# Squares to ScalarE, subtractions and wide sums to VectorE, and an order planned with a shared port, in a retention and MLP kernel

## The chip, the cores and the metric

The kernel runs on one core of one Trainium2 chip. The metric is the device time of one execution in microseconds; the median of three runs is given. The engines are TensorE (PE), VectorE (DVE), ScalarE (ACT), GpSimd (POOL) and SyncE (SP), which issues the transfers.

## The reference

Attention with decay in place of softmax, then an MLP with a squared ReLU, then a gated MLP with SiLU, all in float32. The 4 x 576 rows of the attention are the 2304 rows of the MLPs.

```
q, k, v: (4, 8, 576, 64);  x: (2304, 512)
scores = q @ k.T / 8;  Dmat[i, j] = gamma_h ** (i - j) for i >= j, else 0
x = ((scores * Dmat) @ v), heads side by side
h = relu(x @ w_in);  x = (h * h) @ w_out              # d_ff 2048
g = x @ w_gate;  x = (g * sigmoid(g) * (x @ w_val)) @ w_out2   # d_ff 1536
```

## The kernel before

Every float32 operand of a product is split into a high and a low part of a form that TensorE multiplies fast, and a product is three matmuls (`three`, lines 200 to 202: high by high, high by low, low by high). A split is a rounding copy on ScalarE (`hi`, line 279) and a subtraction on VectorE (`lo`, line 283); the helper `split` makes both for weights, x parts and activations.

The weights arrive as 64-bit patterns. `round32` turns them into float32 (ScalarE lines 241 and 246, VectorE lines 249 to 261), in `convert1` for the first MLP and `convert2_pair` for the second.

The stages are: attention for the first cells; the first MLP's blocks 0 and 1 (`mlp1_h`, `mlp1_act`, `mlp1_y`) with the rest of the attention between their products; its blocks 2 to 4 (`mlp1_s`); the second MLP in three passes of six tiles of 128 rows. Blocks 2 to 4 and the second MLP use Strassen's scheme, in Winograd's form: seven products instead of eight (`PRODUCTS`), with sums of weights (GpSimd, lines 326 and 405), sums of x (`sub` in `fetch_x1`, line 733, and in `fetch_x`, line 967; T1 to T4) and sums of results.

In `mlp1_s` one turn p makes two hidden blocks of 128 for 512 rows. Products go into two banks; `copy` (line 835: m1, u2, m5) and `add` (line 842) take them out, `relu` (line 848) follows on ScalarE, `square` (line 852) on GpSimd, then `hi` (ScalarE, line 860) and `lo` (VectorE, line 864). Pieces of the output product of the turn before are laid between the products. There are 96 halves of 128x256 to be squared. In blocks 0 and 1 the squares run on ScalarE already (line 669).

In the second MLP, `mlp2_gv` makes one hidden block of a pass in seven products: `copy` (ScalarE, line 1069), sums on VectorE (line 1078 c11; line 1081 c22, which product 6 waits for; line 1084 c12; lines 1094 to 1100 the gate). `act_sum` (GpSimd, line 1156) makes sums of activations; `operand` splits activations into `at` tiles; `o_piece` (lines 1217 to 1219) makes the output products, three tiles at a time, laid between the products of later blocks and, at the end of a pass, in one run. `fetch_x` loads the next pass's x and splits it into `xc` tiles; these are the same buffers that the old pass uses, so that the splitting begins with the last block of a pass. `sums_out` takes the output banks out: P1, P7, P5 and C11 copied by ScalarE (line 1258), U2, C21 and C12 added on VectorE (line 1265), and two wide sums, U3 and C22, over 128x768 in `both` (GpSimd, line 1271); then the stores (line 1278).

The order of each engine's queue is made by a planner before the program is written (`Plan`). Each operation is given with its engine, a cost in us, its dependencies and a rank; `emit` steps through time, takes for each engine the ready operation of the least rank, and writes it. TensorE's own order is a chain that follows the program text (`pe`). The costs set the order, and nothing else: the engines wait on semaphores. Sums that TensorE waits for have rank -3, activations -2, the next pass's x 4, weight conversions over 100.

Of the kernel before, what the change touches and what calls it, by code (L numbers as in the profile page):

```python
# [15 lines left out]
ALU = mybir.AluOpType  # L16
# [27 lines left out]
NA = 10  # L44
LOOK = 0.25
Y_FIRST = (0, 0, 3, 3)
TINY, HUGE = (float(np.uint32(b).view(np.float32)) for b in (0x40000000, 0x4FEFFFFF))
# [17 lines left out]
class Op:  # L65


    __slots__ = ("eng", "us", "fn", "deps", "after", "rank", "kb", "n", "out", "left", "ready", "end", "fill")

    def __init__(self, eng, us, fn, deps, after, rank, kb):  # L70
        self.eng, self.us, self.fn, self.rank, self.kb = eng, us, fn, rank, kb
        self.deps, self.after = list(deps), list(after)
        self.out, self.left, self.ready, self.end, self.fill = [], 0, 0.0, None, None


class Plan:
# [9 lines left out]

    def __call__(self, eng, us, fn, deps=(), rank=0.0, kb=0, key=None, after=()):


        o = Op(eng, us, fn, deps, after, rank, kb)  # L90
        o.n = len(self.ops)
        self.ops.append(o)
        if key is not None:
            self.named[key] = o
        return o

    def emit(self):
        waiting = {}
        for o in self.ops:
            for whole, of in ((True, o.deps), (False, o.after)):  # L100
                for d in of:
                    d = d if isinstance(d, Op) else self.named.get(d)
                    if d is not None and d is not o:
                        o.left += 1
                        d.out.append((o, whole))
            if not o.left:
                waiting.setdefault(o.eng, []).append(o)
        free, lanes, left = {}, 0.0, len(self.ops)
        while left:
            best = None  # L110
            for eng, todo in waiting.items():
                if not todo:
                    continue
                t = free.get(eng, 0.0)
# [12 lines left out]
            left -= 1  # L127
            free[o.eng] = t + o.us
            if o.kb:
                lanes = max(lanes, t + o.us + 1.3) + o.kb / 400.0  # L130
                o.end = lanes + 3.0
            else:
                o.end = t + o.us
            for x, whole in o.out:
                lag = 0.0 if x.eng == o.eng else self.LAG.get(o.eng, 0.08)
                x.ready = max(x.ready, o.end + lag if whole else t + 0.01)
                x.left -= 1
                if not x.left:
                    waiting.setdefault(x.eng, []).append(x)
# [18 lines left out]
def kernel(ctx: ExitStack, tc: tile.TileContext, units, qtab, tab, w1, w2, out):  # L158
# [75 lines left out]
    def round32(box, rank, apart=False):  # L234
# [29 lines left out]
        o2 = do("ACT", 1.16, a2, [box["load"] if apart else o1, *r_users[-1:]], rank)  # L264
        p1 = do("DVE", 1.0 if apart else 0.8, d1, [o1], rank)
        p2 = do("DVE", 1.0 if apart else 0.8, d2, [p1], rank)
        p3 = do("DVE", 0.87, d3, [o2] if apart else [p2, o2], rank)
        raw_free = do("NONE", 0.0, lambda: None, [o1, o2, p3])
        do.named["raw", box["n"]] = raw_free
        converts.append(o1)  # L270
        p4 = do("DVE", 1.34, d4, [p2, p3, o2], rank)
        r_users.append(p4)
        return st, p4

    def split(get, n, out, place, rank, deps, cols=None):
# [9 lines left out]
        h = do("ACT", 0.17 + 0.43 * n / 512, hi, deps, rank)  # L285
        return do("DVE", 0.16 + 0.53 * n / 512, lo, [h], rank)

# [25 lines left out]
    def convert_s(p, rank):  # L313
# [15 lines left out]
        ld = do("SP", 0.4, load, [wf_saved[p], f_users[-2]], rank - 20, kb=512, after=raw_loads[-1:])  # L329
        x = do("POOL", 0.87, add(2, 3, 2, ALU.add), [ld], rank)  # L330
        x = do("POOL", 0.87, add(3, 0, 3, ALU.subtract), [x], rank)
        x = do("POOL", 0.87, add(0, 2, 0, ALU.subtract), [x], rank)
        x = do("POOL", 0.87, add(1, 1, 0, ALU.subtract), [x], rank)

# [13 lines left out]
    def convert2_pair(box, f, rank, plain, summed, steps):  # L348
# [31 lines left out]
        def lo2():  # L380
# [5 lines left out]
                    [("xbdone", NB - 1), ("ysv", NB - 2)] if home == "xs" else [("ysv", NB - 1)])  # L386
        front = lambda: do("DVE", 0.69, lo(low, 0, n), [h, *low_free], rank)
        back = lambda: do("DVE", 0.43, lo(rest, n, 768), [h], rank)
        if steps is GV_SUMS:
# [12 lines left out]
        for o, x, y, op in steps:  # L402
            def add(o=o, x=x, y=y, op=op):
                w = st["fm"].rearrange("p (s n) -> p s n", s=4)
                nc.gpsimd.tensor_tensor(out=w[:, o], in0=w[:, x], in1=w[:, y], op=op)  # L405
            l = do("POOL", 0.87, add, [l if o != steps[0][0] else need[o], need[o]], rank)
        h = do("ACT", 1.03, hi2, [l], rank)
        l = do("DVE", 1.22, lo2, [h], rank)
        e = w_dram[summed, f]
# [97 lines left out]
    def att_prep(c, rank):  # L507
# [10 lines left out]
        if c not in FIRST:  # L518
            qs_op[c] = do("POOL", 1.45, qs, [A_op[c], Q_op[c]], rank, after=[ks_op[c - 1]])
        if c not in LAST:  # L520
            ks_op[c] = do("POOL", 1.25, ks, [V_op[c], tab_op], rank, after=[qs_op[c]])

# [133 lines left out]
    def mlp1_act(j, f):  # L656
# [30 lines left out]
        c = do("ACT", 0.19 + 0.43 * k, hi, [b, y_op.get(order1[i - 2]) if i > 1 else None], -2)  # L687
        hlo_op[j, f] = do("DVE", 0.16 + 0.53 * k, lo, [c], -2)

# [29 lines left out]
    def fetch_x1(j, rank):  # L719
# [10 lines left out]
        def sub(o, a, c, deps):  # L730
            eng, us = ("DVE", 0.69) if o in ("T1", "T2") else ("POOL", 1.5)
            e = nc.vector if eng == "DVE" else nc.gpsimd
            return do(eng, us, lambda: e.tensor_tensor(out=at(o), in0=at(a), in1=at(c), op=ALU.subtract), deps, rank)

# [60 lines left out]
    def mlp1_s(j, p, pieces):  # L795
# [55 lines left out]
        def square(key, half):  # L851
            return lambda: nc.gpsimd.tensor_tensor(out=st[key][:, half], in0=st[key][:, half], in1=st[key][:, half], op=ALU.mult)  # L852

        def finish(key, f, half, deps):
# [10 lines left out]

            r = do("POOL", 0.87, square(key, half), deps, -2)
            h = do("ACT", act, hi, [r, y_op.get(order1[i - 2])], -2)
            return do("DVE", 0.58, lo, [h], -2)

# [3 lines left out]
        c11 = name("s11", do("DVE", dve, add("g0", lo_half, "MB", "m1", True), [N_op[j, p, 1], m1, hlo_op.get((j, 2 * p - 3))], -3))  # L873
        r0 = do("ACT", act, relu("g0", lo_half), [c11], -2)
        e0 = finish("g0", f0, lo_half, [r0])
# [8 lines left out]
        c22 = name("s22", do("DVE", dve, add("g1", hi_half, "MA", "m5", True), [N_op[j, p, 4], m5, hlo_op.get((j, 2 * p - 2))], -3))  # L884
        r1 = do("ACT", act, relu("g1", hi_half), [c22], -2)
        e1 = finish("g1", f1, hi_half, [r1])
        product(5, "MB", [m5])
        c12 = name("s12", do("DVE", dve, add("g0", hi_half, "MB", "u2", False), [N_op[j, p, 5], u2], -3))
        r0 = do("ACT", act, relu("g0", hi_half), [c12], -2)
        e0 = finish("g0", f0, hi_half, [r0, e0])  # L890
        hlo_op[j, f0] = e0
        y(take_y[2])
        product(6, "MA", [c22])
        c21 = name("s21", do("ACT", act, relu("g1", lo_half, "MA"), [N_op[j, p, 6]], -3))
        hlo_op[j, f1] = finish("g1", f1, lo_half, [c21, e1])
        y(take_y[3])
# [53 lines left out]
    def fetch_x(b, rank):  # L950
# [14 lines left out]

        def sub(o, a, c):
            return lambda: nc.gpsimd.tensor_tensor(out=at(o), in0=at(a), in1=at(c), op=ALU.subtract)

# [16 lines left out]

        parts_in_order(part, lambda *a, deps: do("POOL", 2.4, sub(*a), deps, min(rank, 4) if b else rank), ld)
        do.named["ysdone", b] = x_chain[-1]
# [59 lines left out]
    def mlp2_gv(s, pieces):  # L1047
# [76 lines left out]
        sg = do("ACT", act, sig(0, lo_half), [c11_, ("si2", s - 1)], -2)  # L1124
        si1 = name("si1", do("DVE", dve, silu(0, lo_half), [sg], -2))
        other(0)
# [11 lines left out]
        sg = do("ACT", act, sig(1, hi_half), [c12_, sg], -2)  # L1138
        si2 = name("si2", do("DVE", dve, silu(1, hi_half), [sg], -2))
        t2_ = name("t2", do("DVE", dve, t2, [si2, c22_], -2))  # L1140
        other(2)
# [9 lines left out]
    def act_sum(b, q, out, x, y, op, deps, rank=-2):  # L1151
# [5 lines left out]

        s_op[b, q, out] = do("POOL", 1.18, go, deps, rank)

# [81 lines left out]
    def sums_out(b):  # L1241
# [27 lines left out]
        def both(name, dst, src, deps):  # L1269
            def go():  # L1270
                nc.gpsimd.tensor_tensor(out=box(dst), in0=box(dst), in1=box(src), op=ALU.add)
            c_op[b, name] = do("POOL", 2.9, go, deps, -3)

# [294 lines left out]
```

## Time and profile before

| | us |
|---|---|
| median of 3 runs | 888.45 (888.36 to 889.59) |
| the profiled execution | 887.93 |
| its span, first to last instruction | 886.1 |
| TensorE busy in it | 865.6 |
| VectorE busy | 639.2 |
| ScalarE busy | 471.6 |
| GpSimd busy | 354.5 |

The span is what the trace shows of the profiled execution; 1.8 us of its time lie around it. TensorE's busy time is a union of overlapping matmuls, so what it lacks to the span is time in which no matmul ran; it does not show whether the clock was at its full or its half level, which is in the column of the granted clock.

### The profile page before, as it was taken

Reading aid. Unit: us, or ns where it says so; the run is one execution under the profiler, and the core shown is the slowest. Engines: PE = TensorE matmul, PEld = TensorE weight load, DVE = VectorE, ACT = ScalarE, POOL = GpSimd, SP = SyncE. Lnnn points to the kernel's source line nnn. Section 1 sums busy time; section 2 is a strip of 40 time slices with the busy share of each in tenths; the row PEclk is TensorE's granted clock in tenths of the full one; section 3 lists DMA queues with packets and bytes.
Section 4 is the critical chain, followed back from the end, with each engine's and each line's share of the span. In section 5 each row is a group of like instructions: output and inputs, shape, how many; then the busy total and the mean of one; then the engine's idle time right before and its main releaser. Section 6 shows DMA issues by size and latency. Waiting matters only on the chain.

```text
span 886.1 us, 15973 instructions
## 1 busy us (share of the span) xinstructions
PE 865.6 (98%) x5995; PEld 809.3 (91%) x5995; DVE 639.2 (72%) x938; ACT 471.6 (53%) x898; POOL 354.5 (40%) x333
## 2 busy tenths in 40 slices
PE   9799999999999999999999999989999989999998
PEld 7688878999899899989999999989999989999998
DVE  4899895637878978897887878596555587555565
ACT  2767674347667667676564544463333354333353
POOL 4131205653646566556581434252122144221231
PEclk9999999999999999999999999999999999999999
DMA  9777868998989698879889998959777767775772
GB/s 359 259 272 269 313 218 258 398 375 282 367 285 352 245 344 315 289 238 341 319 311 323 301 417 317 348 196 330 273 254 259 266 206 259 262 276 214 260 261 74
DMA packets 113085, 254.84 MB, mean 288 GB/s; under 512 B 8560, under 2 KB 67696, under 8 KB 103664
## 3 DMA queue, kind: packets, MB, share of 16 engines
q1 hardware_dynamic: 113008, 253.82, 81.2%
q8 instruction: 47, 0.77, 0.3%
q14 instruction: 30, 0.25, 0.1%
HBM read 195.59 MB, written 58.20 MB: 286 GB/s over the span
## 4 chain that ended last, share of the span: by engine, by line
PE 76%; DVE 13%; issue 3%; DMA 3%; ACT 3%; POOL 2%; SPq 0%; ACTq 0%; POOLq 0%; DVEq 0%
PE gv L200 12%; PE gv L201 12%; PE gv L202 12%; PE acc L201 6%; PE acc L202 6%; PE acc L200 6%; DVE at L283 4%; PE acc L1219 3%; PE acc L1217 3%; PE acc L1218 3%; PE hps L200 3%; PE hps L202 2%; PE hps L201 2%; PE sc L528 1%; PE xs L568 1%
## 5 line engine op out<-in xcount | busy, mean ns | idle before, releaser
L200 PE MATMUL gv<-xc,w 128*128 128x384 f32 x504 | 171.6, 340 | 6.5 <-DVE m L1081 5.7
L201 PE MATMUL gv<-xc,w 128*128 128x384 f32 x504 | 170.3, 338 | 0.0
L202 PE MATMUL gv<-xc,w 128*128 128x384 f32 x504 | 170.0, 337 | 0.0
L201 PE MATMUL acc<-h,w 128*128 128x512 f32 (+1 forms) x320 | 117.8, 368 | 1.1 <-DVE h L679 0.8
L202 PE MATMUL acc<-h,w 128*128 128x512 f32 (+1 forms) x320 | 117.6, 368 | 0.2
L852 POOL TENSOR_TENSOR g<-g 128x256 f32<-128x256 f32 x96 | 86.8, 913 | 77.2 <-ACT g L848 76.5
L200 PE MATMUL acc<-h,w 128*128 128x512 f32 (+1 forms) x320 | 117.3, 367 | 0.0
L200 PEld LDWEIGHTS gv<-xc,w 128*128 128x128 f32 x504 | 94.9, 188 | 9.2 <-DVE m L1081 7.0
L201 PEld LDWEIGHTS gv<-xc,w 128*128 128x128 f32 x504 | 95.3, 189 | 0.2
L202 PEld LDWEIGHTS gv<-xc,w 128*128 128x128 f32 x504 | 95.0, 189 | 0.0
L1219 PE MATMUL acc<-w,at 128*128 128x256 f32 x288 | 81.6, 283 | 0.0
L1218 PE MATMUL acc<-w,at 128*128 128x256 f32 x288 | 81.3, 282 | 0.0
L1217 PE MATMUL acc<-w,at 128*128 128x256 f32 x288 | 81.2, 282 | 0.0
L1069 ACT COPY m<-gv 128x384 f32<-128x384 f32 x72 | 34.6, 481 | 83.1 <-PE gv L202 81.9
L1156 POOL TENSOR_TENSOR st<-g,rs 128x384 f32<-128x384 f32 x18 | 21.7, 1204 | 141.1 <-DVE rs L1100 141.1
L405 POOL TENSOR_TENSOR f<-f 128x256 f32<-128x256 f32 x72 | 66.2, 919 | 29.2 <-DVE cw L362 18.4
L202 PEld LDWEIGHTS acc<-h,w 128*128 128x128 f32 x320 | 60.1, 188 | 10.9 <-DVE w L283 1.0
L864 DVE TENSOR_TENSOR h<-g,h 128x256 fp32r<-128x256 f32 x96 | 62.6, 652 | 7.6 <-ACT h L860 7.5
L200 PE MATMUL gv<-xb,w 128*128 128x256 f32 x238 | 67.2, 282 | 0.8 <-ACT m L835 0.4
L201 PEld LDWEIGHTS acc<-h,w 128*128 128x128 f32 x320 | 60.1, 188 | 8.6 <-DVE h L679 1.3
L201 PE MATMUL gv<-xb,w 128*128 128x256 f32 x238 | 66.9, 281 | 0.1
L202 PE MATMUL gv<-xb,w 128*128 128x256 f32 x238 | 66.8, 281 | 0.0
(175 smaller groups left out, 2246.4 us busy)
## 6 DMA issues: line engine op xcount, KB each, us to landing
w<-wdS SPq DMA_DIRECT2D x36, 1024.0 KB, 5.6
raw<-w SPq DMA_DIRECT2D x34, 1024.0 KB, 7.3
w<-wdP SPq DMA_DIRECT2D x36, 768.0 KB, 7.0
w<-ws SPq DMA_DIRECT2D x94, 256.0 KB, 4.9
w<-wdOP SPq DMA_DIRECT2D x54, 256.0 KB, 4.8
w<-wdOS SPq DMA_DIRECT2D x18, 768.0 KB, 7.4
ws<-cw SPq DMA_DIRECT2D x16, 512.0 KB, 7.2
wdS<-cw SPq DMA_DIRECT2D x12, 512.0 KB, 5.3
```

The source lines that it names most:

```text
L200: nc.tensor.matmul(ps, lhsT=wh, rhs=xh, start=first, stop=False, skip_group_check=onto)
L201: nc.tensor.matmul(ps, lhsT=wh, rhs=xl, start=False, stop=False, skip_group_check=onto)
L202: nc.tensor.matmul(ps, lhsT=wl, rhs=xh, start=False, stop=last, skip_group_check=onto)
L283: nc.vector.tensor_tensor(out=t[:, 1], in0=get(), in1=t[:, 0].bitcast(F32), op=ALU.subtract)
L405: nc.gpsimd.tensor_tensor(out=w[:, o], in0=w[:, x], in1=w[:, y], op=op)
L852: return lambda: nc.gpsimd.tensor_tensor(out=st[key][:, half], in0=st[key][:, half], in1=st[key][:, half], op=ALU.mult)
L864: nc.vector.tensor_tensor(out=t[:, 1, half], in0=st[key][:, half], in1=t[:, 0, half].bitcast(F32), op=ALU.subtract)
L1069: nc.scalar.copy(out=st[name], in_=late[bank][:, :HALF])
L1156: nc.gpsimd.tensor_tensor(out=o, in0=i, in1=k, op=op)
L1217: nc.tensor.matmul(ps, lhsT=ah, rhs=wh, start=product not in ONTO and q == 0 and off == 0, stop=False, skip_group_check=True)
L1218: nc.tensor.matmul(ps, lhsT=ah, rhs=wl, start=False, stop=False, skip_group_check=True)
L1219: nc.tensor.matmul(ps, lhsT=al, rhs=wh, start=False, stop=q == NQ - 1, skip_group_check=True)
```

## The change

The squares of the first MLP's blocks 2 to 4 move from GpSimd to ScalarE, as a second activation right behind the ReLU (`gate`). The x subtractions T3 and T4 of `fetch_x1` and all four of `fetch_x` move from GpSimd to VectorE, and so do the wide sums U3 and C22 at the end of each pass (`both`). The planner learns that GpSimd and some of VectorE's operations (`lock`: those with two inputs in SBUF and some others) slow each other: while both run, each proceeds at the fraction that `SHARE` gives, and an operation that was already placed on the other engine is put off accordingly (`grow`). With that, several costs that held a mean of the slowed times are lowered: weight sums from 0.87 to 0.75 us, activation sums from 1.18 to 1.02, the steps of `round32` and the attention's GpSimd products likewise. Besides what is shown, `lock=True` is set on the low parts of all splits, on `silu` and on `t2`. The products, their order on TensorE and the transfers are not edited.

```diff
+SHARE = {"DVE": 0.5, "POOL": 0.62}
...
-    __slots__ = ("eng", "us", "fn", "deps", "after", "rank", "kb", "n", "out", "left", "ready", "end", "fill")
-
-    def __init__(self, eng, us, fn, deps, after, rank, kb):
+    __slots__ = ("eng", "us", "fn", "deps", "after", "rank", "kb", "n", "out", "left", "ready", "end", "fill", "lock")
+
+    def __init__(self, eng, us, fn, deps, after, rank, kb, lock):
         self.eng, self.us, self.fn, self.rank, self.kb = eng, us, fn, rank, kb
         self.deps, self.after = list(deps), list(after)
-        self.out, self.left, self.ready, self.end, self.fill = [], 0, 0.0, None, None
+        self.out, self.left, self.ready, self.end, self.fill, self.lock = [], 0, 0.0, None, None, lock or eng == "POOL"
...
-        free, lanes, left = {}, 0.0, len(self.ops)
+        free, lanes, left, run = {}, 0.0, len(self.ops), {}
+
+        def grow(o, end):
+            for x, whole in o.out:
+                if whole:
+                    x.ready = max(x.ready, x.ready if x.end else end + (0.0 if x.eng == o.eng else 0.08))
+            o.end = free[o.eng] = end
+
...
+            if o.lock:
+                other = run.get("POOL" if o.eng == "DVE" else "DVE")
+                us = o.us
+                if other and other[0].end > t + 1e-9:
+                    x, since, both, left_x = other
+                    left_x -= max(0.0, min(t, both) - since) * SHARE[x.eng] + max(0.0, t - max(both, since))
+                    first = min(us / SHARE[o.eng], left_x / SHARE[x.eng])
+                    ends = [t + first + max(0.0, w - first * SHARE[e]) for w, e in ((us, o.eng), (left_x, x.eng))]
+                    grow(x, ends[1])
+                    run[x.eng] = x, t, t + first, left_x
+                    run[o.eng] = o, t, t + first, us
+                    free[o.eng] = ends[0]
+                else:
+                    run[o.eng] = o, t, t, us
             if o.kb:
                 lanes = max(lanes, t + o.us + 1.3) + o.kb / 400.0
                 o.end = lanes + 3.0
             else:
-                o.end = t + o.us
+                o.end = free[o.eng]
...
-        p1 = do("DVE", 1.0 if apart else 0.8, d1, [o1], rank)
-        p2 = do("DVE", 1.0 if apart else 0.8, d2, [p1], rank)
-        p3 = do("DVE", 0.87, d3, [o2] if apart else [p2, o2], rank)
+        p1 = do("DVE", 0.69, d1, [o1], rank, lock=True)
+        p2 = do("DVE", 0.69, d2, [p1], rank, lock=True)
+        p3 = do("DVE", 0.75, d3, [o2] if apart else [p2, o2], rank, lock=True)
...
-        p4 = do("DVE", 1.34, d4, [p2, p3, o2], rank)
+        p4 = do("DVE", 1.24, d4, [p2, p3, o2], rank)
...
-        x = do("POOL", 0.87, add(2, 3, 2, ALU.add), [ld], rank)
+        x = do("POOL", 0.75, add(2, 3, 2, ALU.add), [ld], rank)
...
-            eng, us = ("DVE", 0.69) if o in ("T1", "T2") else ("POOL", 1.5)
-            e = nc.vector if eng == "DVE" else nc.gpsimd
-            return do(eng, us, lambda: e.tensor_tensor(out=at(o), in0=at(a), in1=at(c), op=ALU.subtract), deps, rank)
+            eng, us = ("DVE", 0.69)
+            return do(eng, us, lambda: nc.vector.tensor_tensor(out=at(o), in0=at(a), in1=at(c), op=ALU.subtract), deps, rank, lock=True)
...
-            return lambda: nc.gpsimd.tensor_tensor(out=st[key][:, half], in0=st[key][:, half], in1=st[key][:, half], op=ALU.mult)
+            return lambda: nc.scalar.activation(out=st[key][:, half], in_=st[key][:, half], func=ACTF.Square)
+
+        def gate(key, half, deps, bank=None):
+            r = do("ACT", act, relu(key, half, bank), deps, -3 if bank else -2)
+            return r, do("ACT", act, square(key, half), [r], -2)
...
-            r = do("POOL", 0.87, square(key, half), deps, -2)
-            h = do("ACT", act, hi, [r, y_op.get(order1[i - 2])], -2)
-            return do("DVE", 0.58, lo, [h], -2)
+            h = do("ACT", act, hi, [*deps, y_op.get(order1[i - 2])], -2)
+            return do("DVE", 0.42, lo, [h], -2, lock=True)
...
-        r0 = do("ACT", act, relu("g0", lo_half), [c11], -2)
+        _, r0 = gate("g0", lo_half, [c11])
...
-        c21 = name("s21", do("ACT", act, relu("g1", lo_half, "MA"), [N_op[j, p, 6]], -3))
-        hlo_op[j, f1] = finish("g1", f1, lo_half, [c21, e1])
+        c21, r1 = gate("g1", lo_half, [N_op[j, p, 6]], "MA")
+        name("s21", c21)
+        hlo_op[j, f1] = finish("g1", f1, lo_half, [r1, e1])
...
-        def sub(o, a, c):
-            return lambda: nc.gpsimd.tensor_tensor(out=at(o), in0=at(a), in1=at(c), op=ALU.subtract)
+        def sub(o, a, c, deps):
+            eng, us = ("DVE", 0.96)
+            return do(eng, us, lambda: nc.vector.tensor_tensor(out=at(o), in0=at(a), in1=at(c), op=ALU.subtract), deps, min(rank, 4) if b else rank, lock=True)
...
-        parts_in_order(part, lambda *a, deps: do("POOL", 2.4, sub(*a), deps, min(rank, 4) if b else rank), ld)
+        parts_in_order(part, sub, ld)
...
-                nc.gpsimd.tensor_tensor(out=box(dst), in0=box(dst), in1=box(src), op=ALU.add)
-            c_op[b, name] = do("POOL", 2.9, go, deps, -3)
+                nc.vector.tensor_tensor(out=box(dst), in0=box(dst), in1=box(src), op=ALU.add)
+            c_op[b, name] = do("DVE", 0.96, go, deps, -3, lock=True)
```

## Rows read from the trace of the kernel before

**Rows 1.** The page: busy time of each engine, its share, its instructions.

```profile
PE 865.6 (98%) x5995; PEld 809.3 (91%) x5995; DVE 639.2 (72%) x938; ACT 471.6 (53%) x898; POOL 354.5 (40%) x333
```

**Rows 2.** Busy time by stretch: length, each engine, granted clock, transfers' share, GB/s.

```profile
218.00:306.00 88.00, 87.01 (x555) 78.29 (x555) 73.95 (x110) 59.98 (x127) 52.98 (x57) 1.00 0.87 307
...
574.00:607.00 33.00, 29.70 (x219) 29.17 (x219) 29.41 (x37) 19.22 (x40) 16.14 (x9) 0.95 0.66 221
...
713.00:747.00 34.00, 30.66 (x224) 30.14 (x223) 29.52 (x37) 19.32 (x40) 16.95 (x9) 0.95 0.69 217
...
585.00:607.00 22.00, 21.46 (x179) 21.25 (x178) 19.62 (x25) 13.26 (x27) 12.01 (x7) 1.00 0.70 233
...
581.40:584.60 3.20, 3.15 (x11) 3.15 (x12) 2.36 (x4) 0.70 (x2) 0.00 (x0) 0.50 0.44 147
```

**Rows 3.** TensorE's waits: 574:607, 713:747, 218:482, 482:574, 0:218; total, times, longest.

```profile
PE gv L200 <- DVE m L1081: 2.8, 1, 2.8
PE hps L1217 <- DVE oc L1265: 0.5, 1, 0.5
...
PE gv L200 <- DVE m L1081: 2.7, 1, 2.7
PE hps L1217 <- DVE oc L1265: 0.6, 1, 0.6
...
PE gv L200 <- ACT m L835: 0.4, 1, 0.4
...
PE hps L200 <- DVE g L842: 0.2, 1, 0.2
...
PE gv L200 <- DVE rs L1078: 0.4, 1, 0.4
...
PE gv L200 <- DVE m L1081: 0.2, 1, 0.2
...
PE hps L201 <- DVE x L600: 1.8, 1, 1.8
```

**Rows 4.** TensorE's timeline about 580 us: start, duration, instruction, idle before it.

```profile
578.36 0.34 PE L202 MATMUL gv<-xc,w 128*128 128x384 f32 x1
581.46 0.69 PE L200 MATMUL gv<-xc,w 128*128 128x384 f32 x1 [2.76 <-DVE m L1081]
```

**Rows 5.** VectorE's timeline, 573.8 to 582.4 us.

```profile
574.34 0.95 DVE L283 TENSOR_TENSOR xc<-ys,xc 128x768 fp32r<-128x768 f32 x1
575.20 0.56 DVE L283 TENSOR_TENSOR at<-st,at 128x384 fp32r<-128x384 f32 x1
575.67 5.26 DVE L283 TENSOR_TENSOR at<-rs,at 128x384 fp32r<-128x384 f32 x4
580.85 0.55 DVE L1081 TENSOR_TENSOR m<-gv,m 128x384 f32<-128x384 f32 x1
```

**Rows 6.** GpSimd's timeline in the same stretch.

```profile
575.37 4.21 POOL L967 TENSOR_TENSOR ys<-ys 128x768 f32<-128x768 f32 x2 [2.13 <-DVE xc L283]
```

**Rows 7.** An undisturbed block, 566 to 571 us: line 1081 and product 6's first matmul.

```profile
568.25 0.56 DVE L1081 TENSOR_TENSOR m<-gv,m 128x384 f32<-128x384 f32 x1 [1.23 <-PE gv L202]
...
569.03 0.34 PE L200 MATMUL gv<-xc,w 128*128 128x384 f32 x1
```

**Rows 8.** Groups by line and shape, GpSimd and ScalarE: busy, mean ns, idle before.

```profile
L852 POOL TENSOR_TENSOR g<-g 128x256 f32<-128x256 f32 x96 | 86.8, 913 | 77.2 <-ACT g L848 76.5 <-DMA wdS<-f 0.3
...
L967 POOL TENSOR_TENSOR ys<-ys 128x768 f32<-128x768 f32 x9 | 19.2, 2129 | 5.5 <-DVE xc L283 5.2
...
L669 ACT ACTIVATE r<-r 128x256 f32<-128x256 f32 x16 | 6.7, 419 | 0.5
```

**Rows 9.** Timeline of the program's end: a wide sum, a split beside it, the last sum.

```profile
875.20 4.16 POOL L1271 TENSOR_TENSOR oc<-oc 128x768 f32<-128x768 f32 x2 [11.16 <-DVE oc L1265]
...
875.45 2.21 DVE L283 TENSOR_TENSOR at<-rs,at 128x384 fp32r<-128x384 f32 x1
...
883.10 0.43 DVE L1265 TENSOR_TENSOR oc<-acc,oc 128x256 f32<-128x256 f32 x1 [1.45 <-issue]
```

More of the change, by code (lines that the diff above doesn't have):

```diff
@@ L85, in __init__, with __call__ @@
         self.ops, self.named = [], {}
-    def __call__(self, eng, us, fn, deps=(), rank=0.0, kb=0, key=None, after=()):
-        o = Op(eng, us, fn, deps, after, rank, kb)
+    def __call__(self, eng, us, fn, deps=(), rank=0.0, kb=0, key=None, after=(), lock=False):
+        o = Op(eng, us, fn, deps, after, rank, kb, lock)
         o.n = len(self.ops)
@@ L285, in split @@
         h = do("ACT", 0.17 + 0.43 * n / 512, hi, deps, rank)
-        return do("DVE", 0.16 + 0.53 * n / 512, lo, [h], rank)
+        return do("DVE", 0.16 + 0.53 * n / 512, lo, [h], rank, lock=True)
     def convert1(box, f, rank, deps):
@@ L329, in convert_s @@
         ld = do("SP", 0.4, load, [wf_saved[p], f_users[-2]], rank - 20, kb=512, after=raw_loads[-1:])
-        x = do("POOL", 0.87, add(2, 3, 2, ALU.add), [ld], rank)
-        x = do("POOL", 0.87, add(3, 0, 3, ALU.subtract), [x], rank)
-        x = do("POOL", 0.87, add(0, 2, 0, ALU.subtract), [x], rank)
-        x = do("POOL", 0.87, add(1, 1, 0, ALU.subtract), [x], rank)
+        x = do("POOL", 0.75, add(2, 3, 2, ALU.add), [ld], rank)
+        x = do("POOL", 0.75, add(3, 0, 3, ALU.subtract), [x], rank)
+        x = do("POOL", 0.75, add(0, 2, 0, ALU.subtract), [x], rank)
+        x = do("POOL", 0.75, add(1, 1, 0, ALU.subtract), [x], rank)
         def store():
@@ L386, in convert2_pair @@
                     [("xbdone", NB - 1), ("ysv", NB - 2)] if home == "xs" else [("ysv", NB - 1)])
-        front = lambda: do("DVE", 0.69, lo(low, 0, n), [h, *low_free], rank)
-        back = lambda: do("DVE", 0.43, lo(rest, n, 768), [h], rank)
+        front = lambda: do("DVE", 0.69, lo(low, 0, n), [h, *low_free], rank, lock=True)
+        back = lambda: do("DVE", 0.43, lo(rest, n, 768), [h], rank, lock=True)
         if steps is GV_SUMS:
@@ L405, in add @@
                 nc.gpsimd.tensor_tensor(out=w[:, o], in0=w[:, x], in1=w[:, y], op=op)
-            l = do("POOL", 0.87, add, [l if o != steps[0][0] else need[o], need[o]], rank)
+            l = do("POOL", 0.75, add, [l if o != steps[0][0] else need[o], need[o]], rank)
         h = do("ACT", 1.03, hi2, [l], rank)
-        l = do("DVE", 1.22, lo2, [h], rank)
+        l = do("DVE", 1.22, lo2, [h], rank, lock=True)
         e = w_dram[summed, f]
@@ L518, in att_prep @@
         if c not in FIRST:
-            qs_op[c] = do("POOL", 1.45, qs, [A_op[c], Q_op[c]], rank, after=[ks_op[c - 1]])
+            qs_op[c] = do("POOL", 1.27, qs, [A_op[c], Q_op[c]], rank, after=[ks_op[c - 1]])
         if c not in LAST:
-            ks_op[c] = do("POOL", 1.25, ks, [V_op[c], tab_op], rank, after=[qs_op[c]])
+            ks_op[c] = do("POOL", 1.04, ks, [V_op[c], tab_op], rank, after=[qs_op[c]])
     def att_scores(c, rank, fill=None):
@@ L687, in mlp1_act @@
         c = do("ACT", 0.19 + 0.43 * k, hi, [b, y_op.get(order1[i - 2]) if i > 1 else None], -2)
[L688 removed]
+        hlo_op[j, f] = do("DVE", 0.16 + 0.53 * k, lo, [c], -2, lock=True)
     io_users, io_alloc = [], []
@@ L884, in mlp1_s @@
         c22 = name("s22", do("DVE", dve, add("g1", hi_half, "MA", "m5", True), [N_op[j, p, 4], m5, hlo_op.get((j, 2 * p - 2))], -3))
-        r1 = do("ACT", act, relu("g1", hi_half), [c22], -2)
+        _, r1 = gate("g1", hi_half, [c22])
         e1 = finish("g1", f1, hi_half, [r1])
@@ L888, in mlp1_s @@
         c12 = name("s12", do("DVE", dve, add("g0", hi_half, "MB", "u2", False), [N_op[j, p, 5], u2], -3))
-        r0 = do("ACT", act, relu("g0", hi_half), [c12], -2)
+        _, r0 = gate("g0", hi_half, [c12])
         e0 = finish("g0", f0, hi_half, [r0, e0])
@@ L1124, in mlp2_gv @@
         sg = do("ACT", act, sig(0, lo_half), [c11_, ("si2", s - 1)], -2)
-        si1 = name("si1", do("DVE", dve, silu(0, lo_half), [sg], -2))
+        si1 = name("si1", do("DVE", dve, silu(0, lo_half), [sg], -2, lock=True))
         other(0)
@@ L1138, in mlp2_gv @@
         sg = do("ACT", act, sig(1, hi_half), [c12_, sg], -2)
-        si2 = name("si2", do("DVE", dve, silu(1, hi_half), [sg], -2))
-        t2_ = name("t2", do("DVE", dve, t2, [si2, c22_], -2))
+        si2 = name("si2", do("DVE", dve, silu(1, hi_half), [sg], -2, lock=True))
+        t2_ = name("t2", do("DVE", dve, t2, [si2, c22_], -2, lock=True))
         other(2)
@@ L1156, in go @@
             nc.gpsimd.tensor_tensor(out=o, in0=i, in1=k, op=op)
-        s_op[b, q, out] = do("POOL", 1.18, go, deps, rank)
+        s_op[b, q, out] = do("POOL", 1.02, go, deps, rank)
     at_chain = []
```

## The prediction

> **What bounds the kernel now.** I read the page first. TensorE is busy in 865.6 of 886.1 us [rows 1], so an edit to VectorE, ScalarE or GpSimd can only win what TensorE stands still, or what it runs at a lower clock. Next the table by stretch [rows 2]. The reader is to see two stretches, 574 to 607 and 713 to 747 us, where TensorE is busy in only 29.7 of 33.0 and 30.7 of 34.0 us and the granted clock is 0.95. These are the ends of the first two passes of the second MLP: the last hidden block, the remaining output pieces, and the next pass's x being split. VectorE is busy in 29.4 and 29.5 us there; it is the engine that is full. In the first stretch the clock row of 581.4 to 584.6 shows 0.50: half speed, right behind the idle time.
>
> Third, TensorE's waits in these stretches [rows 3]: 2.8 and 2.7 us on VectorE's line 1081 (the sum that product 6 needs), 0.5 and 0.6 us on line 1265 (the U2 sum that frees a bank). TensorE's timeline shows the gap itself: the last matmul before it starts at 578.36, the next at 581.46 [rows 4]. The other stretches hold little: four waits of 0.2 to 0.4 us in the first MLP's last blocks (1.1 us together), three of 0.2 to 0.4 us at the start of the second MLP (0.9 us), and nine of 0.4 to 1.8 us in the first 218 us (8.3 us together; most of it stands in the first 40 us, where things are loaded).
>
> Fourth, why line 1081 is late. In VectorE's queue [rows 5] an `at` split alone takes 0.56 us and the next starts 0.47 us behind it (575.20, 575.67). The four that follow take 5.26 us together instead of 4 x 0.47 = 1.9. Exactly over them GpSimd runs two x subtractions, 575.37 to 579.58 [rows 6]. So two subtractions held VectorE up by about 3.35 us, and line 1081, queued behind, started at 580.85. In an undisturbed block the same sum starts at 568.25, just as its product ends, is done at 568.81, and product 6 starts at 569.03 with no gap [rows 7]: it has 0.2 us to spare. The order before thus put the splits rightly by its own costs (0.56 each); what it did not know is that they stand still beside GpSimd.
>
> **The trace and a rule.** The two engines do not share smoothly in the rows: at the end of the program one split that meets GpSimd's wide sum takes 2.21 us [rows 9], where 0.56 is its own time [rows 5]. The new plan instead lets both proceed at fixed fractions (0.5 and 0.62), by which it would take 1.1 us.
>
> The Trainium skill (SBUF — State Buffer, Who interferes with whom) says that a VectorE instruction with two SBUF inputs and a GpSimd instruction that reads SBUF exclude each other for a whole instruction. The 2.21 us agree with it. By that rule the plan's sharing is wrong in each single case, which speaks against the re-planned order; it is the second case below.
>
> **The change, part by part.**
>
> 1. *x subtractions of the second MLP's passes* (four a pass, 12 in all) go from GpSimd to VectorE. On GpSimd they take 2.13 us [rows 8]. On VectorE the nearest row is the x split of the same 128x768 with two SBUF inputs: 0.95 us [rows 5]. At each of the two pass ends VectorE gets 4 x 0.95 = 3.8 us more and loses the holding, 3.35 us for two, so about 6.7 for four. For line 1081: if both subtractions that stood beside it now stand in front of it, it comes 3.35 - 1.9 = 1.45 us earlier; if they don't, it runs when its product ends and all 2.75 us of the wait go. The nearer row is [rows 7]: a plan that is right about VectorE's time puts the sum (rank -3) before splits (-2) and subtractions (4), and it can only find VectorE in the middle of one instruction of up to 0.95 us, 0.2 us of which is spare. I leave 0.4 us of wait. Behind a subtraction in VectorE's queue stand the splits that the output pieces take and lines 1078 to 1100 of the last block; TensorE waits for both. Per pass end 2.35 us, for two 4.7.
> 2. *The clock.* It stayed at 0.50 for about 3.4 us after each of the two gaps: (1 - 0.95) x 33 = 1.65 and x 34 = 1.7 us lost. The 0.5 us wait on line 1265, at 603 us, has no such dip behind it: 585 to 607 us shows 1.00 [rows 2]. With 0.4 us left I take the dips as gone: 3.4 us. Bounds: 0 (a wait over 1 us remains and the clock falls all the same) and 3.4.
> 3. *U2's bank.* U2 stands behind splits in a VectorE that runs late. It was ready before TensorE came for the bank; with VectorE 1 to 3 us earlier I take 0.8 of the 1.1 us; bounds 0 and 1.1.
> 4. *The wide sums U3 and C22* (six) go from GpSimd to VectorE, about 0.95 us each by the same row as the subtractions. No TensorE wait names them. They put 1.9 us on VectorE at 603 to 607, where its own work ends by about 605 and TensorE has third products to do; if that cover were gone, 1.9 us per pass end. In the last pass nothing is won: the last split piece of C12 at 883.10 waits for the last product, not for C22, and the store behind it ends the span [rows 9]. Taken at 0, bounds -1 and +0.5 us of gain.
> 5. *Squares of blocks 2 to 4* (96) go from GpSimd, 0.91 us each, to ScalarE, where a 128x256 square of a plain block takes 0.42 [rows 8]: 96 x 0.42 = 40 us more over 264 us, 13.4 per 88. ScalarE goes from 60.0 to 73 of 88 us [rows 2]. What it must deliver on time are the copies m1, u2 and m5; the output pieces laid between the products cover a copy. On the other side the chain relu, square, hi, lo gets 0.5 us shorter, and no square holds up a `lo` any more. I take the 1.1 us of waits there as halved (0.5), bounds -1.5 and +1.1. If the cover were gone, each square in front of a copy costs TensorE up to 0.42 us.
> 6. *T3, T4 of the first MLP's x* (six) go to VectorE: six, of 128x512 and so each under the 0.95 us of the larger split, in 264 us where VectorE stands at 74 of 88 [rows 2] and loses the holding by 96 squares. 0.
> 7. *The new order*, from other costs and the sharing rule, moves work everywhere, SP's loads and stores with it, the first 218 us included, where nothing else changes. No transfer is added. At the start of the second MLP I take half of the 0.9 us (0.4). In the first 218 us: 0, bounds -2 and +2.
>
> Sum: 4.7 + 3.4 + 0.8 + 0 + 0.5 + 0 + 0.4 = 9.8 us; less 0.4 us for small new waits where VectorE's queue is re-ordered, so 9.4. The profiled execution took 887.93 us (its span 886.1 and 1.8 around it), which gives 878.5. The median of the runs is 0.5 us above it, so I forecast **879.0 us**.
>
> **The rivals.**
>
> *VectorE stays late at the pass ends.* For it: 28 to 29 of 33 us stay busy, the activation sums still run on GpSimd and still hold splits up, and the plan counts that as sharing. Then line 1081 gains only 1.45 us per end, the clock still dips, U2 gains little: about 2 x (1.45 + 0.3) = 3.5 us, 885.0 us. Against it: the activation sums run beside every block, and outside the pass ends line 1081 is waited for once, 0.2 us [rows 3].
>
> *ScalarE becomes the bound in blocks 2 to 4* (the other side). Its queue runs in order, and it holds conversions of 128x1024 between the copies; with 40 us more, a copy comes behind a square and a conversion, TensorE waits for m1, u2 or m5 at line 835, and product 2, 4 or 5 and all behind it shift. It decides once more than 9.4 of the 40 us (24%) land on TensorE; at a third, 13.4 us, the time is 888.45 - 9.4 + 13.4 = 892.5 us. For it: one wait of line 200 on line 835 is there already, 0.4 us [rows 3]. Against it: 83% is not full, and the squares leave the slower engine.
>
> *The gain is given back by the new order.* The 8.3 us of waits in the first 218 us hang on the order of the first conversions, which is planned anew with no edit in that stage; if they doubled, 888.45 - 9.4 + 8.3 = 887.4 us, no change that could be told. For it: these are the largest waits left. Against it: the new costs are nearer to the rows than the old.
>
> **How the numbers follow.** Forecast 0.70, with a range of its own of 876 to 882 us; VectorE late 0.13; given back 0.08; ScalarE 0.09. A measurement of this kernel can tell about 0.2%, 1.8 us, from no change: faster is the first two, 0.83, same 0.08, slower 0.09. All bounds of gain taken together (5.5 + 3.4 + 1.1 + 0.5 + 1.1 + 0.9) and a little of the first 218 us make about 13 us: 875.5 is the low end. The high end takes in the late VectorE, to 886.8; outside lie the last two cases and a few hundredths below.
>
> **What would show it.** Right: no wait of line 200 on line 1081 above 0.6 us, no stretch of clock 0.50 before the end, TensorE's idle time 5 to 6 us less in the two stretches and none at line 1217; GpSimd without lines 967, 733 and 1271; `at` splits of 2.2 us gone, longer ones only beside activation sums; ScalarE near 73 of 88 us in blocks 2 to 4. Wrong: a wait of one us or more on lines 1081 or 835, or new waits before 218 us.

## The result, and the profile after

The changed kernel takes **876.51 us** (median of 4 runs, 875.52 to 877.65) against 888.4 before: a ratio of 0.987, interval 0.985 to 0.989. The forecast was 879.0. Its profiled execution takes 877.47 us, its span 875.5, 10.6 less than before.

Lines have moved by 21 to 26: what was line 1081 is 1107, 1265 is 1291, 1271 is 1297, 967 is 993, 852 is 873, 283 is 305, 679 is 701. TensorE's order is the same matmul by matmul, so that the time between the starts of the same two matmuls can be compared. By stretch, as difference to the kernel before in us (worked out from the traces; the first line gives, for the kernel before, the start of the matmul that bounds the stretch; the second stretch also holds the first block of the second MLP, whose products start at 461.8 us in the kernel before):

```
                    start  first MLP  second MLP  1st pass           2nd pass       end    span
                           2 to 4     starts      ends      between  ends, 3rd
before, up to       218.4    477.9      575.9      609.1     715.4    859.8        886.1   886.1
changed             +2.1   -2.9       -1.1        -5.1      -0.1     -5.2          +1.7   -10.6
```

First the two pass ends, by stretch as in [rows 2]:

```profile
572.00:602.00 30.00, 30.00 (x232) 29.82 (x231) 27.96 (x43) 19.30 (x41) 4.08 (x3) 1.00 0.79 253
...
708.00:738.00 30.00, 30.00 (x232) 29.82 (x232) 27.85 (x43) 18.66 (x38) 4.08 (x3) 1.00 0.77 253
```

TensorE is busy without a gap, at a granted clock of 1.00; VectorE is as full as before. Its timeline there answers to [rows 5]:

```profile
572.43 0.95 DVE L305 TENSOR_TENSOR xc<-ys,xc 128x768 fp32r<-128x768 f32 x1
573.30 0.55 DVE L305 TENSOR_TENSOR at<-st,at 128x384 fp32r<-128x384 f32 x1
573.77 1.49 DVE L305 TENSOR_TENSOR at<-rs,at 128x384 fp32r<-128x384 f32 x3
575.17 0.95 DVE L993 TENSOR_TENSOR ys<-ys 128x768 f32<-128x768 f32 x1
576.04 0.55 DVE L1107 TENSOR_TENSOR m<-gv,m 128x384 f32<-128x384 f32 x1
```

Three splits take 1.49 us, 0.47 apiece, where four took 5.26. One subtraction of 0.95 us stands in front of the sum, and the sum starts 2.2 us behind the end of the first split (576.04 and 573.85; before 5.1, 580.85 and 575.76). In the whole program nine `at` splits took 2.2 us each before; now none takes over 1.4.

The first MLP's blocks 2 to 4, the squares there on ScalarE, and the `lo` behind them, after and before:

```profile
221.00:309.00 88.00, 88.00 (x571) 80.40 (x570) 65.79 (x115) 73.50 (x166) 17.65 (x20) 1.00 0.90 308
```
```profile
L873 ACT ACTIVATE g<-g 128x256 f32<-128x256 f32 x95 | 39.3, 417 | 1.7
...
L889 DVE TENSOR_TENSOR h<-g,h 128x256 fp32r<-128x256 f32 x96 | 44.7, 465 | 21.9 <-ACT h L885 21.3
...
L864 DVE TENSOR_TENSOR h<-g,h 128x256 fp32r<-128x256 f32 x96 | 62.6, 652 | 7.6 <-ACT h L860 7.5
```

ScalarE is at 73.5 of 88 us, as worked out, and TensorE does not stand still; the `lo` takes 0.47 us in place of 0.65. What TensorE waits for in the whole program (its longest waits, and those at the end):

```profile
PE hps L224 <- DVE w L305: 2.0, 1, 2.0
PE spare L577 <- DVE P L559: 1.7, 1, 1.7
PE hps L223 <- DVE x L622: 1.7, 1, 1.7
...
PE acc L1245 <- DVE at L305: 0.6, 1, 0.6
...
PE acc L1243 <- DVE oc L1291: 0.5, 1, 0.5
```

The longest are now all in the first stage. The wait on the split of a weight, 2.0 us at 117 to 119 us, was one of 0.5 us before, and this execution's clock is at 0.50 right behind it:

```profile
118.00:120.70 2.70, 1.44 (x6) 1.23 (x7) 2.67 (x5) 0.00 (x0) 0.00 (x0) 1.00 0.96 215
120.80:124.10 3.30, 3.30 (x9) 2.61 (x8) 0.95 (x1) 1.33 (x3) 1.04 (x1) 0.50 1.05 334
```

VectorE's timeline, after and then before, shows why: the decay products of a later cell (line 559, before 537) stand in front of that split now, 1.3 us, where they stood behind it.

```profile
116.78 1.29 DVE L559 TENSOR_TENSOR P<-sc,dec 128x512 f32<-128x512 f32 x2
117.99 1.21 DVE L305 TENSOR_TENSOR w<-f,w 128x1024 fp32r<-128x1024 f32 x1
...
116.75 1.23 DVE L283 TENSOR_TENSOR w<-f,w 128x1024 fp32r<-128x1024 f32 x1
118.00 1.29 DVE L537 TENSOR_TENSOR P<-sc,dec 128x512 f32<-128x512 f32 x2
```

And the end, VectorE:

```profile
862.78 2.02 DVE L1297 TENSOR_TENSOR oc<-oc 128x768 f32<-128x768 f32 x2
864.90 0.69 DVE L1291 TENSOR_TENSOR oc<-acc,oc 128x512 f32<-128x512 f32 x1
865.51 0.42 DVE L1291 TENSOR_TENSOR oc<-hps,oc 128x256 f32<-128x256 f32 x1
865.84 1.02 DVE L305 TENSOR_TENSOR at<-rs,at 128x384 fp32r<-128x384 f32 x2
```

Both wide sums and two narrower ones (line 1291), 3.1 us of VectorE, stand in front of the last two splits, which TensorE's last products take: the wait of 0.6 us. The wait of 0.5 us behind it is for a sum of line 1291, which frees a bank and stands behind those splits.

### The profile page after: what moved, and what is told of

Its sections match the earlier page's. It is cut to its first block, busy times and chain, and to the rows that moved or that the text cites. A ratio compares the mean times of both kernels' runs of the same rounds, so it can differ in the third digit from the quotient of the medians.

```text
span 875.5 us, 15902 instructions
## 1 busy us (share of the span) xinstructions
PE 861.2 (98%) x5995; PEld 808.2 (92%) x5995; DVE 603.5 (69%) x962; ACT 506.8 (58%) x994; POOL 216.7 (25%) x213
## 4 chain that ended last, share of the span: by engine, by line
PE 91%; DVE 5%; ACT 2%; issue 1%; DMA 1%; DVEq 0%; ACTq 0%
PE gv L222 13%; PE gv L223 13%; PE gv L224 13%; PE acc L224 7%; PE acc L223 7%; PE acc L222 7%; PE acc L1245 4%; PE acc L1243 4%; PE hps L222 4%; PE acc L1244 4%; PE hps L224 4%; PE hps L223 4%; PE sc L550 1%; PE xs L590 1%; PE xs L577 1%; PE hps L1354 1%
## 5 line engine op out<-in xcount | busy, mean ns | idle before, releaser
L427 POOL TENSOR_TENSOR f<-f 128x256 f32<-128x256 f32 x72 | 61.6, 855 | 218.2 <-DVE cw L384 144.2
L224 PEld LDWEIGHTS acc<-h,w 128*128 128x128 f32 x320 | 60.3, 188 | 11.1 <-DVE w L305 1.0
L223 PEld LDWEIGHTS acc<-h,w 128*128 128x128 f32 x320 | 60.4, 189 | 6.9 <-DVE h L701 0.4
L222 PEld LDWEIGHTS acc<-h,w 128*128 128x128 f32 x320 | 60.4, 189 | 6.5
L889 DVE TENSOR_TENSOR h<-g,h 128x256 fp32r<-128x256 f32 x96 | 44.7, 465 | 21.9 <-ACT h L885 21.3
```

The costliest lines, as they stand in the source:

```text
L222: nc.tensor.matmul(ps, lhsT=wh, rhs=xh, start=first, stop=False, skip_group_check=onto)
L223: nc.tensor.matmul(ps, lhsT=wh, rhs=xl, start=False, stop=False, skip_group_check=onto)
L224: nc.tensor.matmul(ps, lhsT=wl, rhs=xh, start=False, stop=last, skip_group_check=onto)
L889: nc.vector.tensor_tensor(out=t[:, 1, half], in0=st[key][:, half], in1=t[:, 0, half].bitcast(F32), op=ALU.subtract)
```

## Experiments

All are measured against the kernel before, in the same runs on the same chip; ratios with 95% intervals. The columns of the table above, for all of them, stand at the end of this section.

**The x subtractions alone.** In the kernel before, with its own planner:

```diff
-            return lambda: nc.gpsimd.tensor_tensor(out=at(o), in0=at(a), in1=at(c), op=ALU.subtract)
+            return lambda: nc.vector.tensor_tensor(out=at(o), in0=at(a), in1=at(c), op=ALU.subtract)
...
-        parts_in_order(part, lambda *a, deps: do("POOL", 2.4, sub(*a), ...
+        parts_in_order(part, lambda *a, deps: do("DVE", 0.96, sub(*a), ...
```

> The kernel before with only the x subtractions of the second MLP's passes moved to VectorE (cost 0.96), its planner untouched. If the subtractions on GpSimd are the cause of the late sum, most of the gain at the two pass ends is here: 879 to 882 us, and no clock of 0.50 inside the program. If the sharing in the planner is needed as well, about half: 883 to 886 us.

878.98 us, ratio 0.990 (0.987 to 0.993), just under the first range: the pass ends are 5.0 and 5.1 us shorter, all that the whole change wins there, and the span is 9.7 us shorter, of the 10.6 of the whole change. The second MLP's start is 1.4 us longer than before. A clock of 0.50 does occur, at 29 us (last section), but at neither pass end. By stretch:

```profile
569.00:602.00 33.00, 33.00 (x252) 32.77 (x251) 29.27 (x47) 21.58 (x43) 9.10 (x5) 1.00 0.78 249
705.00:738.00 33.00, 33.00 (x252) 32.77 (x251) 28.25 (x45) 21.53 (x43) 10.98 (x6) 1.00 0.76 249
```

No sharing in the planner is needed for this: freed of GpSimd, VectorE's real times are those that the old plan had assumed.

**The x subtractions back**, in the changed kernel (`eng, us = ("POOL", 1.84)`, GpSimd in place of VectorE).

> The changed kernel with the four x subtractions of a pass of the second MLP on GpSimd again (cost 1.84). If GpSimd's subtractions are what holds line 1081 up, the waits and the clock at 0.50 return: 3 to 5 us at each of two pass ends, 882 to 887 us. If a planner that knows of the sharing is enough, the sum is placed in front of the held splits: under 2 us slower, 876 to 878.5 us.

883.84 us, ratio 0.996 (0.994 to 0.997). VectorE and GpSimd at the first pass end:

```profile
575.98 4.30 DVE L305 TENSOR_TENSOR at<-rs,at 128x384 fp32r<-128x384 f32 x2
580.21 0.55 DVE L1107 TENSOR_TENSOR m<-gv,m 128x384 f32<-128x384 f32 x1
...
575.68 4.19 POOL L993 TENSOR_TENSOR ys<-ys 128x768 f32<-128x768 f32 x2 [2.48 <-DVE xc L305]
```

The holding is back: two splits take 4.30 us for 1.0. By the planner's fraction they would take 2.2; they take as long as the two subtractions beside them, 4.19. This is what the prediction said against the plan's sharing. TensorE waits 2.2 and 1.8 us for line 1107; the clock falls to 0.50 behind the first wait and not behind the second. The sharing planner puts two splits fewer in front of the sum than the old one did, and the pass ends are 1.3 and 3.3 us shorter than before, not 5: half a remedy.

**The planner alone**: the changed planner and costs, with squares (0.62 us), subtractions (1.84 in the second MLP, 1.29 for T3 and T4) and wide sums (1.84) on GpSimd.

> The changed kernel with its planner (sharing, new costs), but with squares, x subtractions and wide sums back on GpSimd at unheld costs. If the gain comes from taking the x subtractions off GpSimd, the pass ends lose again about 4 us each: 884 to 889 us, with line 1081's counterpart waited for by over 1 us. If the gain comes from the planner, which now places that sum with the holding in mind, most stays: 877 to 881 us.

901.85 us, ratio 1.016 (1.014 to 1.019): slower than either theory had it. The pass ends win 3.2 and 2.5 us, but the first MLP's blocks 2 to 4 lose 19 us. **The squares back**, the changed kernel with line 873 on GpSimd (cost 0.62), shows the same by itself.

> The changed kernel with the 96 squares on GpSimd again (cost 0.62 and shared). The first MLP's blocks 2 to 4 came out 2 to 3 us shorter; if the squares on ScalarE did that, waits of 0.2 to 0.5 us return there and it takes 878 to 880 us. If the new order or the T3 and T4 subtractions did it, it stays at 876 to 877.5 us.

898.32 us, ratio 1.012 (1.009 to 1.014), also beyond both theories. TensorE's longest wait, and VectorE's and SyncE's timelines around it:

```profile
PE gv L222 <- DMA sx<-ws: 13.8, 1, 13.8
```
```profile
443.72 1.22 DVE L384 TENSOR_TENSOR sx<-f,cw 128x512 fp32r<-128x512 f32 x1
...
444.97 0.32 SPq L331 DMA_DIRECT2D wdP<-sx  x1
...
451.20 0.38 SPq L803 DMA_DIRECT2D sx<-ws  x1
```

A conversion of the second MLP's weights makes its low part in a buffer (`sx`) that the weight sums of block 4 are then loaded into. The load may go only when the last of 13 such conversions has stored. Here that one is made at 443.7 us; before, at 414.9, in the changed kernel at 416.7 (shown in this order):

```profile
414.87 0.69 DVE L362 TENSOR_TENSOR sx<-f,cw 128x512 fp32r<-128x512 f32 x1
...
416.75 0.68 DVE L384 TENSOR_TENSOR sx<-f,cw 128x512 fp32r<-128x512 f32 x1
```

The load goes 6.2 us after the store, in SyncE's queue right behind another store of the same conversion. Behind the wait the clock is at 0.50 for 13.6 us, in which TensorE works 3.5, and once more for 3.4 us. My reading is that with the squares on GpSimd the sharing planner takes VectorE for fuller than it is and puts the conversions, its lowest rank, off by 27 us. VectorE did have room: it is busy 68.6 and 66.0 of 88 us in 221 to 309 and 309 to 397 us, where in the kernel before it was busy 74.1 and 75.1. The plan's own times were not looked at.

**The squares alone**: the kernel before, its planner untouched, `square` as an activation with the cost of the others.

> The kernel before with only the 96 squares moved to ScalarE, its planner untouched. If the squares do no more than end small waits in the first MLP's blocks 2 to 4: 885.5 to 888 us, and the weight conversions there end about where they did. If ScalarE becomes the bound: above 890 us, with waits on its copies. If conversions come earlier and shorten more: below 885 us.

887.11 us, ratio 0.999 (0.997 to 1.000). Blocks 2 to 4 get 2.4 us shorter, and the conversions stay (414.8 us); 1.1 us of it go again at the start of the second MLP. The whole time differs too little to be told from the kernel before. So the squares are worth 2.4 us in their own stage, of the 2.9 that the whole change wins there, and under the sharing planner their move is what keeps the conversions on time. T3 and T4 were not tried alone.

**All moves without the sharing**: the changed kernel with the sharing off and the old costs for what is not moved.

> The changed kernel with all moves, but no sharing in the planner and the costs of before for what is not moved. If the moves carry the change, the pass ends are as in the changed kernel and the first 218 us are as before, where the new order lost about 2 us: 873.5 to 877 us. If the sharing is what places the sum rightly: 880 to 884 us, with waits on it at the pass ends.

880.78 us, ratio 0.992 (0.989 to 0.994): between the theories. The pass ends are within 0.6 us of the changed kernel's, the start is 3 us shorter. But TensorE waits 2.4 us for the x of the second MLP (lines 301 and 305), at 459 to 466 us, which makes the stretch that ends at 477.9 us 0.9 us longer than before, although the products of blocks 2 to 4 in it are done 2.3 us sooner; and it waits 1.3 us for a sum behind two splits and a conversion. The sharing, with its costs, does place this work better; it does not place the pass ends better.

**The wide sums back** (`do("POOL", 1.84, ...)` in `both`).

> The changed kernel with U3 and C22 on GpSimd again (cost 1.84). My reading of the end is that the wide sums on VectorE stand in front of two splits that the last products need, 1.1 to 1.7 us: without them 874.5 to 876 us, and no wait for a split at the end. If the wide sums on VectorE are worth something, because on GpSimd they hold splits up, it is slower: 878 to 881 us.

876.55 us, ratio 0.987 (0.986 to 0.989): the same as the changed kernel within what can be told. In the trace the pass ends are as short (5.1 and 4.8 us) and the end loses 0.3 in place of 1.7 us, but of these 1.4 us nothing shows in the median. The forecast of 874.5 to 876 was missed by half a us.

**Mending.** Three edits of the changed kernel: the first stage in its old order (`if o.lock and t > 200`, and the costs of before in `round32` for the first MLP, `att_prep` and `convert_s`); U3 and C22 in the last pass behind the splits (`-1 if last else -3`); both.

> The changed kernel with the first stage's order of before alone (sharing from 200 us of plan time on, that stage's costs of before). If the new order of the first stage costs 2 to 4 us: 872.5 to 874.5 us, the stage up to 218 us about 3 us shorter than in the changed kernel. If what was gained together with the later wide sums came from the end: 875.5 to 877 us.

> The changed kernel with rank -1 for U3 and C22 in the last pass alone. If the two splits behind the wide sums cost 1.2 us at the end, one of the two waits there (on the split, 0.6 us) goes and it is 0.5 to 1.3 us faster: 875 to 876 us. If the end is bound by the last products anyway: 876 to 877 us.

> The changed kernel with two mendings: the planner shares only from 200 us of its own time on, with the costs of before for the first stage (so that stage has the order of before), and in the last pass U3 and C22 have rank -1, behind the splits. If the new order lost 2 us in the first stage and the wide sums 1.2 to 1.7 us at the end: 871.5 to 874 us. If the loss of the first stage is only spread between executions: 874 to 876 us.

In the order of these texts: the start alone 874.99 us (ratio 0.986, 0.985 to 0.988), between its two ranges; the end alone 874.73 us (0.986, 0.985 to 0.988), a little better than its first range, with the wait on the split gone, and a start that happened to be 2.5 us shorter than the changed kernel's in the profiled execution; both 873.36 us (0.983, 0.981 to 0.986), in its first range. By the ratios neither alone can be told from the changed kernel. With both, TensorE's waits for the last 30 us are one:

```profile
PE acc L1243 <- DVE oc L1291: 0.5, 1, 0.5
```

The first stage in its old order, with the wide sums on GpSimd in all passes, ends this one too:

> The first stage's order of before, and U3 and C22 on GpSimd in all passes (cost 1.84). If the wide sums on VectorE were worth nothing at the pass ends and cost 1.2 to 1.7 us at the end: 872 to 873.5 us, the fastest. If GpSimd's sums hold splits that matter: 874.5 us or more.

873.37 us, ratio 0.984 (0.983 to 0.986), in the first range, and as fast as both mendings together. These two versions are the fastest: their runs lie between 872.75 and 873.93 us, those of the changed kernel between 875.52 and 877.65, 3.1 us of median. They were not measured beside the changed kernel, and the intervals of the ratios still touch.

**A plan in which the engines take turns** (`SHARE = {"DVE": 0.001, "POOL": 1.0}`).

> The changed kernel with a planner in which VectorE's locked operations stand still while GpSimd has one (fractions 0.001 and 1.0 for 0.5 and 0.62). If the sharing at fractions misplaces operations because the engines in truth take turns, the order gets better: 1 us or more faster, 873 to 875.5 us. If only the sum of the two times matters to the order, it is within 1.5 us of the changed kernel, either way.

893.85 us, ratio 1.007 (1.006 to 1.009): wrong by both theories. The first pass end is as short as in the changed kernel (5.2 us won), the second 0.8 us longer (4.4 won); the first 218 us lose 10.3, most of it in one wait of 7.1 us up to 179 us:

```profile
177.55 1.04 ACT L301 CAST cw<-fs 128x1024 fp32r<-128x1024 f32 x1 [6.37 <-POOL fs L348]
178.50 0.38 ACT L687 ACTIVATE r<-hps 128x256 f32<-128x256 f32 x1
178.98 1.12 PE L584 MATMUL hps<-kv 128*64 128x64 f32 x16 [7.09 <-issue]
```

TensorE's sums of line 584 need the bank that the ReLU of line 687 takes out; they are given that ReLU as a dependency in the program. It stands in ScalarE's queue behind a rounding that waits 6.4 us for GpSimd's weight sums. My fractions let GpSimd go first even where VectorE came first, so this settles nothing on turn-taking; it shows how much the first stage hangs on the order.

```
                    start  first MLP  second MLP  1st pass           2nd pass       end    span
                           2 to 4     starts      ends      between  ends, 3rd
changed             +2.1   -2.9       -1.1        -5.1      -0.1     -5.2          +1.7   -10.6
planner alone       +0.4   +19.2      -1.0        -3.2      +0.6     -2.5          -0.0   +13.5
x back              +3.2   -3.0       -0.3        -1.3      +0.5     -3.3          +1.7    -2.4
wide sums back      +1.6   -3.0       -1.1        -5.1      +0.3     -4.8          +0.3   -11.8
squares back        -0.4   +17.9      -1.0        -5.1      +0.1     -5.2          +1.7    +8.0
x alone             -0.7   -0.3       +1.4        -5.0      -0.0     -5.1          -0.0    -9.7
squares alone       -0.3   -2.4       +1.1        -1.4      +0.4     +0.3          +0.0    -2.2
moves alone         -1.2   +0.9       +0.7        -5.3      +0.3     -4.6          +1.7    -7.5
both mended         -2.1   -2.9       -1.2        -5.1      +0.2     -4.8          +0.8   -15.1
start mended        -1.6   -3.0       -0.6        -5.1      +0.1     -5.2          +1.7   -13.6
end mended          -0.4   -2.9       -1.1        -5.1      -0.2     -4.8          +0.8   -13.8
start, sums back    -1.4   -2.9       -1.1        -5.1      +0.3     -4.6          -0.0   -14.8
turns               +10.3  +1.7       +0.2        -5.2      +0.8     -4.4          +1.7    +5.0
```

## Why the prediction was right, point by point

*Pass ends (items 1 to 3).* Mechanism and place were right, and shown from both sides: the subtractions alone bring 5.0 and 5.1 us, and back on GpSimd they bring the wait back. The terms were a little small: 8.9 us forecast for sum, clock and U2, 10.3 measured, since none of the 0.4 us that I left per end is waited for (0.8) and U2's wait is gone wholly (0.3 more); the other 0.3 I cannot place. The sum did come behind one subtraction, as allowed for.

*The clock (item 2).* It is 1.00 at both pass ends. In the squares-alone kernel the same 2.7 us wait on line 1081 occurs at both, but the clock falls only behind the second; the first pass end is 1.4 us shorter than before, the second 0.3 longer:

```profile
572.00:606.00 34.00, 30.71 (x234) 30.19 (x233) 29.88 (x38) 20.19 (x41) 17.58 (x9) 1.00 0.71 231
712.00:747.00 35.00, 31.72 (x231) 31.20 (x230) 29.40 (x38) 18.25 (x37) 17.24 (x9) 0.95 0.68 220
```

So the dip is worth about what the term said, 1.4 to 1.7 us, but it does not follow every such wait.

*Squares (item 5).* The load of ScalarE, 73.5 of 88, was right and it did not become the bound. The gain was mis-sized: 0.5 us forecast, 2.9 measured for the stretch (2.4 with the squares alone). I had added up the listed waits, 1.1 us. A listed wait is only what is left after the modelled end of the matmul before it. In the trace of before:

```profile
223.13 0.28 PE L202 MATMUL hps<-xb,w 128*128 128x256 f32 x1
223.76 0.39 PE L200 MATMUL gv<-xb,w 128*128 128x256 f32 x1 [0.34 <-DVE g L842]
223.98 0.28 PE L201 MATMUL gv<-xb,w 128*128 128x256 f32 x1
```

The two starts are 0.63 us apart where 0.12 is usual, and the next start comes 0.10 us late as well: 0.61 us lost for 0.34 listed. Six starts that are late by 0.2 to 0.5 us and the small steps beside them make 3.5 us between 217 and 482 us.

*The wide sums (item 4).* Taken at 0 with a bound of 1 us of loss; they cost 1.4 to 1.7 us at the end of the profiled executions. With the start mended, putting them behind the splits or back on GpSimd lowers the median by 1.6 us (874.99 to 873.36 and 873.37). That is beyond the bound. The step that failed is "In the last pass nothing is won", with the loss taken at 0: I looked at what the sums wait for, not at what is queued behind them, the last two splits. At the pass ends they are worth nothing either way: on GpSimd these ends are within 0.6 us of as short.

*The order (item 7).* At the second MLP's start half of the 0.9 us was forecast, 1.1 measured. By the runs this comes with the sharing planner: the planner alone wins 1.0 there, and without the sharing the moves lose 0.7 (all moves), 1.4 (x alone) and 1.1 us (squares alone).

The first 218 us were taken at 0 with bounds of 2; the profiled execution lost 2.1, and its clock's dip is worth up to 1.7 of that. One execution proves little here. The seven kernels of this document that have the queues' order of before up to 208 us start between 2.1 us faster and level with the kernel before (1.0 faster in the mean); the six that have the changed kernel's order up to 211 us lie between 0.4 faster and 3.2 slower (1.1 slower in the mean). All six have the wait of 2.0 us on the weight's split, where the kernel before has 0.5. So the new order costs about 2 us there, and the order of before, put back, lowers the median by 1.4 to 3.2 us in three pairs (start mended and changed, both mended and end mended, start with sums back and wide sums back), though these were not measured side by side.

Two of the signs named in the prediction came out against it in this stage: a clock of 0.50 before the end, and a new wait before 218 us, which it lists as a sign of being wrong. The others held in the main; but TensorE still waits 0.5 us at line 1243 (before 1217), in the last pass, and two of the longer splits, of 1.1 us, stand beside weight sums.

Luck has a part in how close the sum came, as the errors partly cancel: 1.4 more at the pass ends, 2.4 more in blocks 2 to 4 and 0.7 at the second MLP's start, less 2.1 at the start and 1.7 at the end, and with the 0.4 us kept for new waits and 0.1 between the passes, make the 1.2 us by which the span's gain of 10.6 exceeds the 9.4. The median gains 11.9.

*The rivals.* VectorE late at the pass ends: not here; it is what x back shows. ScalarE as the bound: no. The gain given back by the new order: at most a fifth of it; but with the squares on GpSimd the new order would have made the kernel 10 us slower than before, by a way that I had not named, a buffer freed late by a low-rank conversion.

## What to carry to other kernels

When a plan's times hold for each engine alone, look for two engines that hold each other up before changing the plan: moving 12 instructions off GpSimd did what a planner that modelled the holding as a sharing did only half. A new cost model re-orders every stage, so measure it stage by stage, apart from the moves, and keep the old order where it was better. For work moved into a queue, name what stands behind it there, at the program's end above all, where nothing else covers it.

## What the runs showed that I had not expected

The clock's fall is not certain. In the profiled executions of seven of these kernels (x back, x alone, squares alone, moves alone, both mended, start mended, turns) the granted clock is 0.50 for 3.4 us from 29 to 31 us on, in the first six of them behind a wait of 1.6 to 2.0 us on an x split. In the profile of before it stays at 1.00 there behind the same wait of 1.8 us [rows 3], and in those of the changed kernel and of the one with the wide sums back behind 1.7. The wait of 2.0 us at 117 to 122 us is in all six kernels with the changed kernel's first stage; the clock falls behind it in three (changed, squares back, end mended) and not in the others (planner alone, x back, wide sums back). Why, no run here tells. Two single starts that differ by 1.7 us are therefore no evidence about their order, and single profiled executions are compared by stretch above for that reason.
